# Second layer of an attention and expert kernel: the first rows ahead of the layer's start, v scaled by a constant, outputs in float16

## The chip, the cores and the metric

One core of a Trainium2 chip runs the whole program. The metric is the time of one execution on the device in microseconds (us); the kernel before takes 884.76 us, the median of three runs.

## The reference

```python
def reference(q, k, v, f, moe_*, moe2_*):
    x = decayed causal attention of q, k, v, f       # 4 batches, 8 heads, 576 rows, width 64
    x = x.transpose(...).reshape(4, 576, 512)
    u = x + (x.T @ U @ V).T                           # mixing of rows, rank 32
    y = u + max(u @ w_ch1, 0) @ w_ch2                 # 512 -> 2048 -> 512
    logits = y @ w_gate                               # 4 experts, the best two are kept
    for e in range(4):
        a = causal softmax(y @ wq[e] @ (y @ wk[e]).T / 8)
        out += weight[e] * (a @ (y @ wv[e]) @ wo[e])
```

All inputs are float32 and the result is wanted to nearly that accuracy. So each large product is made three times, from a high and a low half of both factors (high by high, high by low, low by high).

## The kernel before, in words

The program has three stages: the attention of the first layer (to about 200 us) and its row mixing, the feed-forward part, and the second layer, in which each of 4 batches has 4 expert heads (16 heads in all, from about 672 us on).

**Feed-forward.** The hidden width is worked in four quarters. A step is one quarter of one half (288 rows) of a batch. It makes 4 hidden tiles (`hps`, 12 matmuls of 288 columns each; ScalarE writes the high half `hh`, VectorE the low half `hl`), and the matmuls of step i's outputs (`cps`) alternate with the hidden tiles of step i+1. The input `ust` of a step is split in two parts (`cast_some`): ScalarE writes `uh`, and the low half `ul` is `ust` minus `uh`. The outputs of the last quarter, `yc`, are the second layer's input y. For each batch `largest_y` and `finish_y` look for the largest magnitude of y in each partition, turn the maximum over the partitions into a power of two, and write y times that factor as float16 halves `yh` and `yl` to `yhalves` in DRAM, from where `load_y` brings them in for the second layer. For batches 0 to 2 the maximum over the partitions goes through TensorE (`power`). For the last batch `power_aside` sends the 128 values to DRAM (`mdram`) and reads them back as a row in every partition (`mrow`).

**Second layer.** For a batch, `experts_qk(b, pair)` makes q and k of two heads (48 `pq` matmuls of 288 columns); ScalarE and VectorE each write one half of every result, times `back`, the product of the factors that were taken out. `expert_values` makes v and the gate's logits (60 `pv` matmuls of 260 columns). `head_max` makes the bound of each row's scores in three parts: products `ua`, products `ub`, and the transposition `mt`; it ends in a row `mr`, which is put by DMA beside q. A head's scores `sc` are made in two pieces, ScalarE takes their exponentials `pf`, GpSimd masks the diagonal (`affine_select`), ScalarE and VectorE split them into `ph` and `pl`, and one head later come the products `av` with v. `expert_out` transposes a batch's outputs (`op`), splits them in `oh` and `ol`, and makes the products `po` with wo (512 columns), which go out from `ost`.

**v in the kernel before.** ScalarE copies each `pv` to `vr` (L1340), VectorE takes the largest magnitude (`bm`, L1341). When all five tiles are there, `batch_scale` makes one power of two (`bsp`, `bs`), ScalarE scales the whole `vr` (L1319) and writes the high half `vh` (L1320), and GpSimd makes the low half `vl` in four subtractions (L1322).

**Order.** In the feed-forward part TensorE, VectorE and ScalarE (and the transfer queue of SyncE) execute the instructions in the order in which the program is written. In the second layer only TensorE does; the order on ScalarE, VectorE and GpSimd there is set by the framework's scheduler when the program is built. `work_on(n)` advances queued generators (`work`) by n pieces between the fixed parts of a head. A piece that ends in `LATER` is not counted, so several may follow in one place. Products with a result in PSUM take three buffers in turn (pool `psf`: `hps`, `cps`, `pq`, `pv`, `op`, `po`, `mt`), and two more are for `ua`, `ub` and `sc`. A matmul waits until its buffer has been read.

## Time and profile before

| | |
|---|---|
| median of 3 runs | 884.76 us (884.66 to 885.23) |
| profiled execution, its own time | 880.85 us |
| span of its trace | 878.7 us |
| TensorE clock granted, mean (1 is full) | 0.965 |
| busy: TensorE, VectorE, ScalarE, GpSimd | 89%, 73%, 50%, 28% of the span |
| last matmul ends, span ends | 874.7, 878.7 us |
| time by engine of the chain that ended last | TensorE 63%, VectorE 21%, DMA 8%, ScalarE 4% |

The span is the time from the first to the last instruction in the trace. It lies 2.15 us under that execution's own time, and the median of the three runs is 3.9 us above the profiled execution. Changes are therefore worked out in the trace and then taken from the median. In the rows, PE is TensorE, DVE VectorE, ACT ScalarE and POOL GpSimd; L1281 is line 1281 of the kernel; a tile's name stands as out<-in.

### The profile page before, as it was taken

How to read it: one execution, taken by the hardware profiler on the slowest of the kernel's cores; microseconds unless marked ns; L12 is line 12 of the kernel's file. 1: busy time of each engine (PE TensorE's matmuls, PEld its weight loads, DVE VectorE, ACT ScalarE, POOL GpSimd, SP SyncE). 2: the span in 40 equal slices, each digit the busy share in tenths (PEclk: the TensorE clock that was granted, in tenths of full speed). 3: DMA queues.
4: the chain of work that ended last, by engine and by line, in shares of the span. 5: the costliest groups of instructions: out<-in, count | busy, mean ns of one | idle time of the engine just before them, and what ended most of it. 6: DMA issues, size and time to landing. Idle time of an engine off the chain costs nothing.

```text
span 878.7 us, 19044 instructions
## 1 busy us (share of the span) xinstructions
PE 778.8 (89%) x7422; PEld 691.2 (79%) x7422; DVE 642.5 (73%) x1692; ACT 436.8 (50%) x824; POOL 242.3 (28%) x325
## 2 busy tenths in 40 slices
PE   3487487889999999989799999999998689989897
PEld 2477487888999899989799877777776478878786
DVE  6989978986777657646849873775663779877775
ACT  3668566555455554443417331332231367666764
POOL 9856645543433423000200001002004022121210
PEclk9889689999999999999999999999999799999999
DMA  6344565443443431116345323144010531422122
GB/s 185 108 114 137 179 201 164 124 135 96 133 117 91 139 111 48 57 49 208 129 125 184 118 84 116 29 162 151 1 54 1 174 85 27 106 60 66 43 72 84
DMA packets 56617, 93.75 MB, mean 107 GB/s; under 512 B 5024, under 2 KB 36240, under 8 KB 56528
## 3 DMA queue, kind: packets, MB, share of 16 engines
q1 hardware_dynamic: 51968, 83.76, 32.0%
q10 hardware_dynamic: 4560, 8.78, 2.7%
q8 instruction: 58, 0.95, 0.4%
q14 instruction: 31, 0.25, 0.1%
HBM read 53.32 MB, written 21.38 MB: 85 GB/s over the span
## 4 chain that ended last, share of the span: by engine, by line
PE 63%; DVE 21%; DMA 8%; ACT 4%; issue 3%; POOL 0%; SPq 0%; POOLq 0%; DVEq 0%; ACTq 0%
PE cps L634 19%; PE hps L618 18%; PE sc L231 7%; DVE ph L247 4%; PE pv L1337 3%; DVE ub L188 3%; PE po L1379 3%; DMA ust<-udram 2%; DMA raw<-in_w_dram 2%; PE ub L183 2%; PE pq L1266 2%; PE gp L828 2%; PE av L262 1%; PE av L266 1%; PE av L264 1%
## 5 line engine op out<-in xcount | busy, mean ns | idle before, releaser
L622 ACT ACTIVATE hh<-hps 128x288 fp32r<-128x288 f32 (+1 forms) x128 | 52.5, 410 | 208.9 <-PE hps L618 201.6
L247 DVE TENSOR_TENSOR ph<-pf,ph 128x576 f16<-128x576 f32 x144 | 129.0, 899 | 29.9 <-ACT ph L246 29.5
L623 DVE SCALAR_TENSOR_TENSOR hl<-hps,hh 128x288 fp32r<-128x288 f32 (+1 forms) x128 | 58.0, 453 | 76.8 <-ACT hh L622 76.5
L241 ACT ACTIVATE pf<-sc 128x576 f32<-128x576 f32 x144 | 84.1, 612 | 37.7 <-PE sc L231 30.5
L231 PE MATMUL sc<-qa,ka 128*128 128x288 f32 (+4 forms) x288 | 77.2, 329 | 21.8 <-DMA qa<-mr 10.1
L246 ACT CAST ph<-pf 128x576 f16<-128x576 f32 x144 | 89.3, 636 | 5.5 <-POOL pf L243 4.2
L188 DVE CUSTOM_DVE_ANT_0 ub<-ub,maskm 128x448 f32<-128x448 f32 x192 | 81.8, 426 | 11.1 <-PE ub L183 8.9
L634 PE MATMUL cps<-hh,w2h 128*128 128x288 f32 x256 | 79.7, 311 | 0.0
L618 PE MATMUL hps<-uh,w1h 128*128 128x288 f32 x256 | 75.1, 315 | 3.5 <-DVE hl L623 1.6
L634 PE MATMUL cps<-hh,w2l 128*128 128x288 f32 x256 | 76.0, 297 | 0.0
L634 PE MATMUL cps<-hl,w2h 128*128 128x288 f32 x256 | 75.8, 296 | 0.0
L231 PEld LDWEIGHTS sc<-qa,ka 128*128 128x128 f32 x288 | 53.5, 206 | 26.9 <-ACT pf L241 5.7
L262 PE MATMUL av<-vh,ph 128*128 128x65 f16 x720 | 72.3, 197 | 2.0 <-DVE x L311 2.0
L634 PE MATMUL cps<-hl,w2hf 128*128 128x288 f16 x256 | 73.2, 286 | 0.0
L634 PE MATMUL cps<-hh,w2lf 128*128 128x288 f16 x256 | 73.2, 286 | 0.0
L634 PE MATMUL cps<-hh,w2hf 128*128 128x288 f16 x256 | 73.2, 286 | 0.0
L264 PE MATMUL av<-vl,ph 128*128 128x64 f16 x720 | 71.9, 194 | 0.0
L266 PE MATMUL av<-vh,ph 128*128 128x65 f16 x720 | 71.8, 194 | 0.0
L262 PEld LDWEIGHTS <-ph 128*128 128x128 f16 x720 | 66.5, 98 | 5.7 <-DVE x L311 2.1
L618 PE MATMUL hps<-uh,w1l 128*128 128x288 f32 x256 | 71.0, 299 | 0.0
L231 PE MATMUL sc<-qb,kb 128*128 128x288 f32 (+4 forms) x288 | 68.3, 319 | 0.0
L264 PEld LDWEIGHTS <-ph 128*128 128x128 f16 x720 | 66.9, 100 | 0.2
(235 smaller groups left out, 2318.5 us busy)
## 6 DMA issues: line engine op xcount, KB each, us to landing
raw<-in_w_dram SPq DMA_DIRECT2D x32, 512.0 KB
qkt<-in_qk_dram SPq DMA_DIRECT2D x16, 576.0 KB
ust<-udram SPq DMA_DIRECT2D x14, 576.0 KB
vr<-in_v_dram SPq DMA_DIRECT2D x16, 320.0 KB
udram<-ustage ACTq DMA_DIRECT2D x16, 288.0 KB
ydram<-ust SPq DMA_DIRECT2D x8, 576.0 KB
yc<-ydram SPq DMA_DIRECT2D x8, 576.0 KB
qb<-qa SPq DMA_DIRECT2D x24, 144.0 KB
```

Of the source, the lines that this page charges most:

```text
L188: nc.vector.tensor_tensor_reduce(ub[:, bk, off:off + w], ub[:, bk, off:off + w], maskm[:, S - w:S], 1.0, NEG, OP.add, OP.max, mx[:, t:t + 1])
L231: nc.tensor.matmul(ps[:, bk, off:off + w], wa, xa, start=bk not in banks[:n], stop=bk not in banks[n + 1:])
L241: nc.scalar.activation(pfv, view, AF.Exp, scale=ISC)
L246: nc.scalar.copy(ph[:, o0:o0 + n], pf[:, 0:n])
L247: nc.vector.tensor_tensor(pl[:, o0:o0 + n], pf[:, 0:n], ph[:, o0:o0 + n], OP.subtract)
L262: nc.tensor.matmul(av[:, it, :], ph[:, c:c + P], vh[:, jt, :], start=first, stop=False)
L264: nc.tensor.matmul(av[:, it, 0:64], ph[:, c:c + P], vl[:, jt, :], start=False, stop=False)
L266: nc.tensor.matmul(av[:, it, :], pl[:, c:c + P], vh[:, jt, :], start=False, stop=last)
L618: nc.tensor.matmul(ph[:], wa[:, k, fs], xa[:, k], start=n == 0, stop=n == 3 * KT - 1)
L622: nc.scalar.activation(hh[:], ph[:], AF.Relu)
L623: nc.vector.scalar_tensor_tensor(hl[:], ph[:], 0.0, hh[:] if dt == F16 else f32(hh[:]), OP.max, OP.subtract)
L634: nc.tensor.matmul(pc[:], wa[:, t, dsl], xa[:], start=n == 0, stop=n == 3 * FT - 1)
```

## The change

1. `first_rows`: q and k of the first two heads and the row bounds of heads 0 and 1 are made in the last two feed-forward steps instead of behind them.
2. The last batch's y is not split in halves behind the feed-forward part. It is stored as it is (`ydram`), and `last_y` loads it in the second batch's heads (from head 5 on), takes the maximum there, and splits it in four pieces of 576 elements per partition on ScalarE (`yh`) and VectorE (`yl`). Its two small matmuls use the buffers of `psf`. `power_aside` goes.
3. v is scaled by the constant `DOWN`, 2 to the power of -22. ScalarE writes `vh` and the logits `lg` and VectorE writes `vl` for each tile straight from `pv`. The copy, the maximum, `batch_scale` and `batch_parts` go.
4. wo, `oh` and `ol` are float16; wo gets a scale of its own (a third `power`), which a factor in the scaling of `ost` takes back.
5. `cast_some` makes `ul` on VectorE instead of GpSimd.

```diff
+DOWN = 2.0 ** -22
...
-    def power_aside(am, up):
-
-        nc.sync.dma_start(mdram[:], am)
-        full = cur["s16"].tile([P, P], F32, name="mrow", bufs=1)
-        nc.sync.dma_start(full[:], mdram[:].rearrange("p o -> o p").to_broadcast([P, P]))
-        yield
-        es = cur["s16"].tile([P, 2], F32, name="es", bufs=16)
-        nc.vector.tensor_reduce(es[:, 0:1], full[:], AX.X, OP.max)
-        nc.vector.tensor_scalar(es[:, 0:1], es[:, 0:1], 1.0e-30, None, OP.max)
-        nc.vector.tensor_scalar(es[:, 0:1].bitcast(I32), es[:, 0:1].bitcast(I32), 0x7F800000, None,
-                                OP.bitwise_and)
-        nc.vector.tensor_scalar(es[:, 0:1], es[:, 0:1], 1.0 / up, None, OP.mult)
-        nc.vector.reciprocal(es[:, 1:2], es[:, 0:1])
-        return es
...
-            nc.gpsimd.tensor_tensor(dl, sv, f32(dh), OP.subtract)
+            nc.vector.tensor_tensor(dl, sv, f32(dh), OP.subtract)
...
-                if j == KT - 1 and q == 3:
+                if j == KT - 1 and q == 3 and b < B - 1:
...
-    woh = sw.tile([P, 2, DM], F32R, name="woh")
-    wol = sw.tile([P, 2, DM], F32R, name="wol")
+    woh = sw.tile([P, 2, DM], F16, name="woh")
+    wol = sw.tile([P, 2, DM], F16, name="wol")
...
+        parts = [(g, k, wah[:, k, c0:c1], wal[:, k, c0:c1], wraw[:, k, c0:c1])
+                 for k in range(KT) for g, (c0, c1) in enumerate(((0, q1), (q1, NA)))]
+        parts += [(2, k, woh[:, k, :], wol[:, k, :], sts[k][:]) for k in range(2)]
...
+        back, ey = backs[b], st_y[b][:, 0:1]
         for g in range(2):
-            nc.vector.tensor_tensor(backs[b][:, g:g + 1], st_y[b][:, 0:1], st_w[g][:, 0:1], OP.mult)
+            nc.vector.tensor_tensor(back[:, g:g + 1], ey, wscales[:, g:g + 1], OP.mult)
+        nc.vector.scalar_tensor_tensor(back[:, 2:3], back[:, 1:2], 1.0 / DOWN, wscales[:, 2:3],
+                                       OP.mult, OP.mult)
...
-    def batch_scale(am):
-
-        sp = psf.tile([P, NT], F32, name="bsp", tag="f")
-        nc.tensor.matmul(sp[:], every[:], am[:], start=True, stop=True)
-        rs = sy.tile([P, 1], F32, name="bs", bufs=4)
-        nc.vector.tensor_reduce(rs[:], sp[:], AX.X, OP.max)
-        nc.vector.tensor_scalar(rs[:], rs[:], 1.0 / VEXP, 1.0e-30, OP.mult, OP.max)
-        nc.vector.tensor_scalar(rs[:].bitcast(I32), rs[:].bitcast(I32), 0x7F800000, None,
-                                OP.bitwise_and)
-        nc.vector.reciprocal(rs[:], rs[:])
-        yield
-        return rs
-
-    def batch_parts(vr, rs, vh, vl):
-
-        scaled = nc.scalar.mul(vr, vr, rs[:, 0:1])
-        nc.scalar.copy(vh[:, :, :, 0:64], vr)
-        for e in range(E):
-            nc.gpsimd.tensor_tensor(vl[:, :, e], vr[:, :, e], vh[:, :, e, 0:64], OP.subtract)
-        return scaled
...
     def expert_values(b, y):
 
         yh, yl = y
-        vr = sy.tile([P, NT, NV], F32, name="vr3", bufs=1)
         v0 = 2 * E * D
-        am = sy.tile([P, NT], BF16, name="bm")
+        vh = sy.tile([P, NT, E, 65], F16, name="vh3")
+        vl = sy.tile([P, NT, E, 64], F16, name="vl3")
+        nc.gpsimd.memset(vh[:, :, :, 64:65], 1.0)
+        lg = sy.tile([P, NT, E], F32, name="lg3")
         for t in range(NT):
             pv = psf.tile([P, 512], F32, name="pv", tag="f")
             ts_ = slice(t * P, t * P + P)
...
                     nc.tensor.matmul(pv[:, 0:NV], ya[:, k, ts_], wa[:, k, v0:v0 + NV],
                                      start=n == 0, stop=n == 3 * KT - 1)
                     n += 1
-            nc.scalar.mul(vr[:, t, :], pv[:, 0:NV], backs[b][:, 1:2])
-            nc.vector.tensor_reduce(am[:, t:t + 1], vr[:, t, 0:E * D], AX.X, OP.max,
-                                    apply_absolute_value=True)
-            yield
-        vh = sy.tile([P, NT, E, 65], F16, name="vh3")
-        vl = sy.tile([P, NT, E, 64], F16, name="vl3")
-        nc.gpsimd.memset(vh[:, :, :, 64:65], 1.0)
-        vv_ = vr[:, :, 0:E * D].rearrange("p t (e d) -> p t e d", e=E)
-        yield LATER
-        scale = batch_scale(am)
-        next(scale)
-        yield LATER
-        rs = drain(scale)
-        st_v[b] = (vh, vl, rs, sy.tile([P, E, NT], F32, name="cf", bufs=2))
-        first = batch_parts(vv_, rs, vh, vl).ins
-        gating.append(gates(vr[:, :, E * D:NV], st_v[b][3]))
+            pe_ = pv[:, 0:E * D].rearrange("p (e d) -> p e d", e=E)
+            nc.scalar.mul(vh[:, t, :, 0:64], pe_, DOWN)
+            last = nc.scalar.mul(lg[:, t, :], pv[:, E * D:NV], backs[b][:, 1:2]).ins
+            nc.vector.scalar_tensor_tensor(vl[:, t], pe_, DOWN, vh[:, t, :, 0:64], OP.mult,
+                                           OP.subtract)
+            yield
+        st_v[b] = (vh, vl, sy.tile([P, E, NT], F32, name="cf", bufs=2))
+        gating.append(gates(lg[:], st_v[b][2]))
         if b == 0:
-            with tc.issue_after(first):
+            with tc.issue_after(last):
                 drain(gating.pop())
...
-        oh = sy.tile([P, 2, S], F32R, name="oh", bufs=1)
-        ol = sy.tile([P, 2, S], F32R, name="ol", bufs=1)
+        oh = sy.tile([P, 2, S], F16, name="oh", bufs=1)
+        ol = sy.tile([P, 2, S], F16, name="ol", bufs=1)
...
-            nc.scalar.copy(ost[0:k, :], po[0:k, :])
+            nc.scalar.mul(ost[0:k, :], po[0:k, :], backs[b][0:k, 2:3])
...
+    def last_y(yh, yl):
+
+        b = B - 1
+        halves = [sy.tile([P, KT, HC], F32, name=f"yst{c}", bufs=1) for c in range(NC)]
+        for c in range(NC):
+            nc.sync.dma_start(halves[c][:], ydram[b, :, :, c * HC:c * HC + HC])
+        for t_ in (yh, yl):
+            nc.gpsimd.memset(t_[:, :, S:SP_], 0.0)
+        yield LATER
+        yield LATER
+        am = sy.tile([P, 2 * NC], F32, name="yam", bufs=1)
+        for n in range(2 * NC):
+            k = 2 * (n % 2)
+            nc.vector.tensor_reduce(am[:, n:n + 1], halves[n // 2][:, k:k + 2], AX.XY, OP.max,
+                                    apply_absolute_value=True)
+            yield LATER
+        a1 = sy.tile([P, 1], F32, name="ya1", bufs=1)
+        nc.vector.tensor_reduce(a1[:], am[:], AX.X, OP.max)
+        yield LATER
+        st_y[b] = yield from power(a1[:], UPW, ((psf, "f"), (psf, "f")), LATER)
+        factors_back(b)
+        up = st_y[b][:, 1:2]
+        for c in range(NC):
+            cs = slice(c * HC, c * HC + HC)
+            for k in range(0, KT, 2):
+                dh, dl, sv = yh[:, k:k + 2, cs], yl[:, k:k + 2, cs], halves[c][:, k:k + 2]
+                nc.scalar.mul(dh, sv, up)
+                nc.vector.scalar_tensor_tensor(dl, sv, up, dh, OP.mult, OP.subtract)
+                yield LATER
...
+    def first_rows():
+
+        yield from experts_qk(0, 0, y)
+        yield
+        cur["first_k"] = cur["tmp"].ins
+        rows = [head_max(0), head_max(1)]
+        for m in (0, 1):
+            one(rows[m])
+            yield
+            one(rows[m])
+            yield
+        yield
+        for m in (0, 1):
+            one(rows[m])
+            yield
+
     NH = B * E
+    with tc.manual_schedule(engines=IN_ORDER):
+        jobs.append(second_weights())
+        y = load_y(0, sy0)
+        dense_until(len(steps) - 2)
+        drain(in_turn(*jobs))
+        del jobs[:]
+        for b in range(B - 1):
+            factors_back(b)
+        jobs.append(first_rows())
+        dense_until(len(steps))
+        drain(in_turn(*jobs))
+        del jobs[:]
...
     with tc.manual_schedule(engines={mybir.EngineType.PE}):
-        drain(experts_qk(0, 0, y))
-        first_k = cur["tmp"].ins
         work.append(experts_qk(0, 1, y))
+        work.append(expert_values(0, y))
+        sc = expert_scores(0, 0)
         work_on(2)
-        m0, m1 = head_max(0), head_max(1)
-        one(m0)
-        work_on(1)
-        one(m0)
-        work_on(1)
-        one(m1)
-        work.append(expert_values(0, y))
-        work_on(1)
-        one(m1)
-        work_on(1)
-        one(m0)
-        work_on(3)
-        one(m1)
-        with tc.issue_after(first_k):
+        one(sc)
+        work_on(2)
+        one(sc)
+        work_on(2)
+        with tc.issue_after(cur["first_k"]):
             y_next = load_y(1, ys[1])
         for h in range(NH):
             b, e = divmod(h, E)
             more = b + 1 < B
             if e == 0 and more:
+                if b + 2 == B:
+                    drain(late)
                 y = y_next
                 work.append(experts_qk(b + 1, 0, y))
-            if e == 1 and b + 2 < B:
+            if e == 1 and b + 2 < B - 1:
                 with tc.issue_after(cur["last"].ins):
                     y_next = load_y(b + 2, ys[b % 2])
+            if e == 1 and b + 2 == B - 1:
+                y_next = [ys[b % 2].tile([P, KT, SP_], F16, name=n) for n in ("yh", "yl")]
+                late = last_y(*y_next)
+                with tc.issue_after(cur["last"].ins):
+                    next(late)
+                work.insert(0, late)
```

Where the change moves instructions is read from the order of each engine's instructions, first on VectorE where the feed-forward part ends and the second layer begins. `yc` is the end of a feed-forward step, the lines with `qb` and `kb` write q and k of the first heads, `es<-mrow` is the last batch's power of two. The kernel before:

```order
L639 SCALAR_TENSOR_TENSOR yc<-cps,back,yc 128x288 x4
L531 TENSOR_REDUCE yam<-yc 128x1 x2
L555 TENSOR_REDUCE ya_9148<-yam 128x1
L1281 SCALAR_TENSOR_TENSOR qb_8332<-pq,back_8320,qa_8331 64x288
L1281 SCALAR_TENSOR_TENSOR qb_8336<-pq,back_8320,qb_8336 64x288
L1281 SCALAR_TENSOR_TENSOR qb_8332<-pq,back_8320,qa_8331 64x288
L543 TENSOR_REDUCE es<-mrow 128x1
L1281 SCALAR_TENSOR_TENSOR qb_8336<-pq,back_8320,qb_8336 64x288
L544 TENSOR_SCALAR es<-es 128x1
```

The changed kernel:

```order
L613 SCALAR_TENSOR_TENSOR hl<-hps,hh 128x288
L1251 SCALAR_TENSOR_TENSOR qb_8332<-pq,back_8320,qa_8331 64x288
L1251 SCALAR_TENSOR_TENSOR qb_8336<-pq,back_8320,qb_8336 64x288
L629 SCALAR_TENSOR_TENSOR yc<-cps,back,yc 128x288
L1251 SCALAR_TENSOR_TENSOR qb_8332<-pq,back_8320,qa_8331 64x288
L1251 SCALAR_TENSOR_TENSOR qb_8336<-pq,back_8320,qb_8336 64x288
L613 SCALAR_TENSOR_TENSOR hl<-hps,hh 128x288
L1251 SCALAR_TENSOR_TENSOR kb_8334<-pq,back_8320,ka_8333 64x288
L1251 SCALAR_TENSOR_TENSOR kb_8338<-pq,back_8320,tmp 64x288
```

The work on the first q and k now stands between `hl` and `yc` of the feed-forward steps, and no instruction that reads `mrow` stands among it.

On ScalarE in the second batch's heads, where q and k of the third batch are made (`qa`, `qb`, `ka`, `tmp`), the kernel before has the two long steps on v:

```order
L1284 ACTIVATE qa_9202<-pq,back_8322 64x288
L241 ACTIVATE pf<-sc 128x512 x2
L1286 ACTIVATE qb_9207<-pq,back_8322 64x288
L1319 ACTIVATE vr_10362<-vr_10362,bs 128x5x256
L246 CAST ph_9238<-pf 128x512
L1284 ACTIVATE qa_9202<-pq,back_8322 64x288
L246 CAST ph_9238<-pf 128x512
L1320 CAST vh_10541<-vr_10362 128x20x64
L1293 ACTIVATE ka_9204<-pq,back_8322 64x288
L1286 ACTIVATE qb_9207<-pq,back_8322 64x288
```

The changed kernel has the four pieces of the last batch's y (`yh<-yst`) there, in the middle of the same eight instructions of q and k:

```order
L1254 ACTIVATE qa_9304<-pq,back_8322 64x288
L1256 ACTIVATE qb_9309<-pq,back_8322 64x288
L1385 ACTIVATE yh<-yst_10278,es 128x2x288 x2
L1385 ACTIVATE yh<-yst_10279,es 128x2x288 x2
L1254 ACTIVATE qa_9304<-pq,back_8322 64x288
L1263 ACTIVATE ka_9306<-pq,back_8322 64x288
L241 ACTIVATE pf<-sc 128x576
L246 CAST ph_9342<-pf 128x576
L1263 ACTIVATE ka_9306<-pq,back_8322 64x288
```

The two steps on v are gone from between the reads of `pq`, and four steps on y stand in one row between the first and the second pair of them.

On VectorE at about 419 to 436 us, where the feed-forward weights of a later quarter are prepared (`w`, `wam`), the changed kernel has the subtractions `ul` in its row, which in the kernel before are GpSimd's:

```order
L613 SCALAR_TENSOR_TENSOR hl<-hps,hh 128x288
L599 TENSOR_TENSOR ul<-ust,uh 128x576
L352 SCALAR_TENSOR_TENSOR w_5791<-raw,w_5791 128x512
L353 SCALAR_TENSOR_TENSOR w_5791<-raw,w_5791 128x512
L438 TENSOR_REDUCE wam<-w_5791 128x1
L627 TENSOR_TENSOR ust<-cps,ust 128x288
L599 TENSOR_TENSOR ul<-ust,uh 128x576
```

Each `ul` stands ahead of the next weights, and behind it wait the low halves `hl` that TensorE needs.

## Rows read from the trace of the kernel before

**Rows 1.** Page, part 1: busy time of each engine, share of the span, instructions.

```profile
PE 778.8 (89%) x7422; PEld 691.2 (79%) x7422; DVE 642.5 (73%) x1692; ACT 436.8 (50%) x824; POOL 242.3 (28%) x325
```

**Rows 2.** Windows: from:to, length, busy time of each engine (instructions), TensorE clock, DMA.

```profile
570.00:664.00 94.00, 94.00 (x774) 75.07 (x773) 60.46 (x142) 28.56 (x58) 5.40 (x13) 1.00 0.25 86
...
678.00:687.00 9.00, 0.00 (x0) 0.00 (x0) 0.81 (x2) 0.35 (x1) 0.00 (x0) 0.62 0.22 56
687.00:703.00 16.00, 13.39 (x95) 10.23 (x96) 14.75 (x43) 8.51 (x16) 0.56 (x2) 0.90 0.68 209
703.00:719.00 16.00, 13.07 (x103) 11.04 (x101) 13.04 (x46) 11.57 (x21) 4.82 (x11) 0.96 0.16 35
719.00:723.00 4.00, 4.00 (x26) 3.30 (x24) 2.28 (x5) 1.97 (x4) 0.29 (x1) 0.74 0.63 154
723.00:779.00 56.00, 51.77 (x625) 45.31 (x624) 49.99 (x157) 40.61 (x73) 14.63 (x40) 1.00 0.30 73
779.00:783.00 4.00, 3.98 (x19) 3.68 (x20) 3.34 (x11) 1.96 (x7) 0.29 (x1) 0.57 0.35 76
...
827.00:831.00 4.00, 4.00 (x20) 3.93 (x21) 3.22 (x12) 2.13 (x5) 0.29 (x1) 0.59 0.34 74
```

**Rows 3.** Chain that ended last: start, us, engine or DMA, tile, line, count.

```profile
674.03 7.35 DMA mdram<-ya
681.40 4.71 DMA mrow<-mdram
687.03 4.72 PE pq L1266 x24
...
783.62 1.48 PE po L1379 x6
...
814.13 1.49 PE pq L1266 x12
```

**Rows 4.** Waits of PE, 671 to 879: total us, times, longest.

```profile
PE pq L1266 <- DVE qb L1281: 9.2, 1, 9.2
PE op L1368 <- DVE qb L1281: 3.4, 2, 1.7
PE mt L193 <- DVE qb L1281: 2.9, 1, 2.9
...
PE op L1368 <- DVE kb L1281: 2.0, 2, 1.0
```

**Rows 5.** Timeline of DVE: start, duration, line, operation, tiles, idle before.

```profile
686.13 0.29 DVE L543 TENSOR_REDUCE es<-mrow 128x1 f32<-128x128 f32 x1 [9.96 <-DMA mrow<-mdram]
```

**Rows 6.** Timeline of ACT, where the second batch's heads run, columns as in group 5.

```profile
771.16 1.36 ACT L1319 ACTIVATE vr<-vr,bs 128x1280 f32<-128x1280 f32 x1
...
773.96 1.26 ACT L1320 CAST vh<-vr 128x1280 f16<-128x1280 f32 x1
```

**Rows 7.** Timeline of DVE at the same place.

```profile
776.09 0.74 DVE L307 TENSOR_TENSOR rn<-rn,cf 128x5 f32<-128x5 f32 x1
```

**Rows 8.** Timeline of POOL at the same place.

```profile
775.31 2.98 POOL L1322 TENSOR_TENSOR vl<-vr,vh 128x320 f16<-128x320 f32 x4 [4.13 <-ACT vh L1320]
```

**Rows 9.** Groups of instructions, 703 to 879: count, busy us, mean ns, idle before.

```profile
L1341 DVE TENSOR_REDUCE bm<-vr 128x1 bf16<-128x256 f32 x19 | 7.9, 417 | 2.8 <-ACT vr L1340 2.4
```

**Rows 10.** Groups of instructions, 640 to 680, columns as in group 9.

```profile
L623 DVE SCALAR_TENSOR_TENSOR hl<-hps,hh 128x288 f16<-128x288 f32 x9 | 4.1, 457 | 8.3 <-ACT hh L622 8.3
...
L566 DVE SCALAR_TENSOR_TENSOR yl<-yc,es,yh 128x576 f16<-128x576 f32 x4 | 3.3, 814 | 0.0
...
L565 ACT ACTIVATE yh<-yc,es 128x576 f16<-128x576 f32 x4 | 3.0, 771 | 1.3 <-DVE es L405 1.3
```

**Rows 11.** A window, as in group 2, in the feed-forward part.

```profile
430.00:435.00 5.00, 4.29 (x34) 4.06 (x33) 4.90 (x9) 3.21 (x6) 2.81 (x2) 1.00 0.00 0
```

**Rows 12.** Timeline of DVE in that window.

```profile
432.83 1.93 DVE L348 SCALAR_TENSOR_TENSOR w<-raw,w 128x512 int32<-128x512 int32 x1
434.79 0.69 DVE L349 SCALAR_TENSOR_TENSOR w<-raw,w 128x512 int32<-128x512 int32 x1
```

More of the change, by code (lines that the diff above doesn't have):

```diff
@@ L146 @@
     ydram = dram.tile([B, P, KT, S], F32, name="ydram")
-    mdram = dram.tile([P, 1], F32, name="mdram")
     yhalves = dram.tile([B, 2, P, KT, S], F16, name="yhalves")
@@ L386, in load_quarter_steps, with power @@
             yield
-    def power(am, up=UP16):
-        at_ = ps1.tile([1, P], F32, name="amt", tag="av")
+    def power(am, up=UP16, where=((ps1, "av"), (ps2, "s2")), pause=None):
+        (p0, tag0), (p1, tag1) = where
+        at_ = p0.tile([1, P], F32, name="amt", tag=tag0)
         nc.tensor.transpose(at_[:], am, ident[:])
@@ L398, in power @@
                                 OP.bitwise_and)
-        yield
-        yield
-        rp = ps2.tile([P, 1], F32, name="rsp", tag="s2")
+        yield pause
+        yield pause
+        rp = p1.tile([P, 1], F32, name="rsp", tag=tag1)
         nc.tensor.matmul(rp[:], every[:], full[:].bitcast(BF16)[:, 1:2], start=True, stop=True)
@@ L557, in finish_y @@
         yield
-        es = yield from (power_aside if b == B - 1 else power)(a1[:], UPW)
+        es = yield from power(a1[:], UPW)
         up = es[:, 1:2]
@@ L1133 @@
     wal = sw.tile([P, KT, NA], F16, name="wal")
-    woh = sw.tile([P, 2, DM], F32R, name="woh")
-    wol = sw.tile([P, 2, DM], F32R, name="wol")
-    backs = [sw.tile([P, 2], F32, name=f"back{b}") for b in range(B)]
+    woh = sw.tile([P, 2, DM], F16, name="woh")
+    wol = sw.tile([P, 2, DM], F16, name="wol")
+    wscales = sw.tile([P, 3], F32, name="wscales")
+    backs = [sw.tile([P, 3], F32, name=f"back{b}") for b in range(B)]
     wide = pool("wide")
@@ L1171, in part @@
                     lambda: nc.vector.scalar_tensor_tensor(dl, sv, up, dh, OP.mult, OP.subtract))
-        yield from behind_by_one([part(k, g) for k in range(KT) for g in range(2)])
-        for k in range(2):
-            nc.scalar.copy(woh[:, k, :], sts[k][:])
-            yield
-            nc.vector.tensor_tensor(wol[:, k, :], sts[k][:], f32(woh[:, k, :]), OP.subtract)
+        yield from behind_by_one([pair(*part) for part in parts])
     def factors_back(b):
+        back, ey = backs[b], st_y[b][:, 0:1]
         for g in range(2):
-            nc.vector.tensor_tensor(backs[b][:, g:g + 1], st_y[b][:, 0:1], st_w[g][:, 0:1], OP.mult)
+            nc.vector.tensor_tensor(back[:, g:g + 1], ey, wscales[:, g:g + 1], OP.mult)
+        nc.vector.scalar_tensor_tensor(back[:, 2:3], back[:, 1:2], 1.0 / DOWN, wscales[:, 2:3],
+                                       OP.mult, OP.mult)
     tie = sw.tile([P, E, E], F32, name="tie")
@@ L1197, in load_y @@
         return yh, yl
-    with tc.manual_schedule(engines=IN_ORDER):
-        jobs.append(second_weights())
-        y = load_y(0, sy0)
-        dense_until(len(steps) - 1)
-        for b in range(B - 1):
-            factors_back(b)
-        dense_until(len(steps))
-    drain(in_turn(*jobs))
-    factors_back(B - 1)
-    wide.release()
-    for p_ in (y16, s16, fy, fh, fu, wy_pool, wx_pool, stage):
-        p_.release()
-    hpool2 = pool("heads3", 1, "right")
-    att = pool("att2", 2, "right")
-    cur["pf"] = att
-    sy = pool("sy", 2, "right")
-    ys = [sy0, pool("sy1", 1, "right")]
-    heads += make_heads(hpool2, NH2B)
-    fill_heads(heads[NH2A:])
-    exps = exponent_tiles(hpool2, 2)
     def gates(lg, cf):
@@ L1397, in last_out @@
     def last_out(b):
-        oh = sy.tile([P, 2, S], F32R, name="oh", bufs=1)
-        ol = sy.tile([P, 2, S], F32R, name="ol", bufs=1)
+        oh = sy.tile([P, 2, S], F16, name="oh", bufs=1)
+        ol = sy.tile([P, 2, S], F16, name="ol", bufs=1)
         osum = sy.tile([P, NT, DM], F32, name="osum", bufs=1)
@@ L1407, in last_out @@
                 if m == 0:
-                    nc.scalar.copy(osum[0:k, t, :], po[0:k, :])
+                    nc.scalar.mul(osum[0:k, t, :], po[0:k, :], backs[b][0:k, 2:3])
                 else:
-                    nc.vector.tensor_tensor(osum[0:k, t, :], po[0:k, :], osum[0:k, t, :], OP.add)
+                    nc.vector.scalar_tensor_tensor(osum[0:k, t, :], po[0:k, :], backs[b][0:k, 2:3],
+                                                   osum[0:k, t, :], OP.mult, OP.add)
                     queue = nc.scalar if t % 2 else nc.sync
@@ L1498 @@
                 work.append(tail)
[L1499 removed]
+            if h:
+                sc = expert_scores(b, e)
             m = head_max(h + 2) if h + 2 < NH else iter(())
```

49 lines of the change are left out of this document (30 added, 19 removed).

## The prediction

> **What bounds the kernel now.** I read the page first: TensorE is busy 89% of the span [rows 1], so the question is where it pauses, and whether this change is at those places. The chain that ended last answers for the start of the second layer. For most of the feed-forward part it is TensorE's own products, and then comes a stretch with no engine in it: 7.35 us of a transfer to `mdram`, 4.71 us of one back as `mrow`, and only then 24 products `pq` [rows 3]. VectorE stands at the instruction that reads `mrow` for 9.96 us [rows 5]; behind it in the program's order are the reads of `pq`, so TensorE waits 9.2 us for a `qb` that needs nothing of `mrow` [rows 4]. The windows show the price: from 678 to 687 TensorE does nothing, and from 687 to 703 it has 13.39 us of work in 16 at a granted clock of 0.90 [rows 2].
>
> The list of TensorE's waits names three more places of the kind: a product waits for its PSUM buffer, which a read of q or k still holds. `op` waits for `qb` twice (3.4 us) and for `kb` twice (2.0), and `mt` once for `qb` (2.9) [rows 4]. The windows at 719, 779 and 827 have a clock of 0.74, 0.57 and 0.59, each right behind such a wait [rows 2]: TensorE was idle, and then ran for some time at the lower of its two levels (1.2 instead of 2.4 GHz). What makes `qb` late is seen on ScalarE and VectorE at about 771 to 777. ScalarE has 1.36 us on `vr` and 1.26 us on `vh` [rows 6], VectorE one operation of 5 elements that takes 0.74 us [rows 7] while GpSimd subtracts `vl` for 2.98 us [rows 8], and q and k stand in line behind them.
>
> **The change part by part.** The sum is over what TensorE loses or works less; all differences are of the profiled execution and are then taken from the median.
>
> *Start of the layer.* Lost now: 9.0 us idle, 16 - 13.39 = 2.6 idle, and 16 x 0.10 = 1.6 at the low clock [rows 2], 13.2 in all. Afterwards nothing reads `mrow`, 48 of the 96 first `pq` products and the bounds of heads 0 and 1 lie inside the last two feed-forward steps, and the first scores can follow the last `cps` at once. The work itself is only moved. What it needs of VectorE there is 8 reads of `pq`, each like an `hl` (0.46 [rows 10]), and the bounds, together some 8 us as an estimate; from 570 to 664 VectorE was busy 60.46 of 94 us [rows 2], so the last two steps have room for it. I leave 0.5 us for a seam, so **-12.7**. If the cover is gone, that is if these reads make TensorE pause in the last steps, the gain sinks towards nothing; that end is a rival.
>
> *v.* The three pauses for `qb` and `kb` cost 3.4 + 2.0 + 2.9 = 8.3 us idle [rows 4] and 4 x (0.26 + 0.43 + 0.41) = 4.4 at the low clock [rows 2], so 12.7. The change takes away what stands in the line: 2.6 us of ScalarE in two blocks, 20 reductions of 0.417 on VectorE [rows 9], 2.98 on GpSimd. It adds `vl` on VectorE, 20 of 256 elements. The nearest row is `hl` of 288 elements, also from PSUM with a subtraction, 0.457 [rows 10], so 0.42 each: VectorE has as much as before. ScalarE has about 0.2 us more per tile for the logits, spread out. I take all three pauses as gone, **-12.7**; the lower end is that they stay, nothing.
>
> *The last batch's y.* Its four ScalarE pieces are of 0.77 us, its four VectorE pieces of 0.81 [rows 10], and its four reductions I take as no longer than these. That is 3.1 us of ScalarE in one row between reads of `pq` in the second batch's heads, the same kind of block that 1.36 + 1.26 us make now. I therefore put one pause back: 3.5 us (the four pieces, and an opening on VectorE) and 4 x 0.43 = 1.7 at the low clock, **+5.2**. The lower end is nothing, when the pieces find a gap. Its load from DRAM is 1.2 MB in a stretch in which the DMA engines are 16 to 30% busy [rows 2] and has several us of room; I cost it at nothing, and it would add its own lateness if head 5 came before it.
>
> *float16 outputs.* A `po` product has 512 columns; six take 1.48 us now, 0.247 each [rows 3]. Float16 products of 288 columns run at 1.49 / 12 = 0.124 [rows 3], so 512 at the same pace take 0.221. 120 of them and the small rest give 120 x 0.026 = **-3.1**. The bounds are no gain and that.
>
> *`ul` on VectorE.* Each is 576 elements, near the 0.81 of `yl` [rows 10], and four come into a stretch in which VectorE is busy 4.90 of 5 us and TensorE 4.29 [rows 11]. At worst all is on the path: +3.2. Against it stands that one weight operation took 1.93 us beside GpSimd's `ul`, while its neighbour of the same size took 0.69 [rows 12]; that 1.2 comes back. I also count some lateness, since `ul` waits in VectorE's order for the landing of `ust` which held up GpSimd alone before: **+1.5**, bounds -1.2 and +4.
>
> The Trainium skill ("SBUF — State Buffer", section "Who interferes with whom") says that VectorE with two inputs in SBUF and GpSimd reading SBUF exclude each other for a whole instruction. The 1.93 us and the 0.74 us above agree. By that rule up to 1.4 us (half of 2.81) could come back at each of four casts, 5.6 instead of 1.2, and the edit would be a gain of some 3 us, for 858.6 in all. The trace shows the collision at one cast, so I stay with +1.5 and give that a tenth of the main case's chance.
>
> The sum: -12.7 - 12.7 + 5.2 - 3.1 + 1.5 = -21.8. With 884.76 that is 863.0. The profiled execution is 880.85, 3.9 under the median, and the changed kernel may have another such distance.
>
> **The rivals.** (1) *VectorE bounds the second layer.* From 723 to 779 it is busy 49.99 of 56 us, hardly less than TensorE's 51.77 [rows 2]. The change takes 7.9 us of reductions off it and adds 8.4 of `vl`, 3.3 of `yl`, 3.3 of reductions of y. Then the pauses go from v to other places, and only the start counts: 884.8 - 12.7 - 3.1 + 1.5 = 870.5, and 873.6 if `po` gains nothing. Against it: TensorE's waits of the second layer that I list are all for q and k behind ScalarE's long steps, not spread over heads. (2) *No pause for the last y.* The scheduler put the pieces where `pq` has buffers to spare: 863.0 - 5.2 = 857.8, or 856 if small waits go as well. (3) *The start isn't covered.* The first q, k and bounds hold up the feed-forward steps by as much as they save: 863.0 + 12.7 = 875.7. (4) *Slower.* With v's maximum gone, every tile of v needs two ScalarE steps and one of VectorE before its PSUM buffer is free, where one copy was enough. If that makes TensorE pause in each of heads 1 to 11 as it does now in three of them, at 12.7 / 3 = 4.2 us, 11 pauses cost 46 us. The rest of the change saves 12.7 + 12.7 + 3.1 - 1.5 = 27, so it decides from the seventh such pause on; with eight the time is 884.8 - 27 + 34 = 892. For it speaks how full VectorE is, against it that each tile has 12 products of its own, which cover such a read. (5) *It does nothing*: one of start and v fails and the other is paid back; I see no single place for it.
>
> **How the numbers follow.** Main case 0.53, 863 with its own range 857 to 868 (the pause of y from 2 to 8 us, `ul` by its bounds). Rival 1 0.21, rival 2 0.15, rival 3 0.05, rival 4 0.04, rival 5 0.02. For 8 in 10 the range needs the main case, rival 2, and most of rival 1: 854 to 873. A measurement of this kernel can tell about 0.2% from no change, 1.8 us. Faster by more: 0.94; within: 0.02; slower: 0.04.
>
> **What the profile of the changed kernel would show.** *Start:* no idle stretch of TensorE between the last `cps` and the first scores, clock 1.00 throughout; idle time before `cps` or `hps` in the last 30 us would speak for rival 3. *v:* no `op` or `mt` waiting for `qb` or `kb` in the first and third batches' heads, and no window of 4 us under 0.9 there. *Last y:* one wait of `pq` or of what follows it for ScalarE's `qa`, `qb` or `ka`, 2 to 4 us, in the second batch's heads, and a window near 0.6 behind it. *`po`:* six in about 1.33 us. *`ul`:* TensorE busy less than 4.2 of 5 us near 430. Wrong would be the forecast above all if VectorE is busy more than 95% in the second layer while TensorE pauses in many heads.

## The result and the profile after

Of the changed kernel four runs gave a median of 873.51 us (867.55 to 874.85), against 884.71 (883.14 to 885.23) for the kernel before: a ratio of 0.986, 95% interval 0.982 to 0.991. Six further runs beside 17 of the kernel before, on another occasion, gave 0.982 (0.979 to 0.986). By these ratios it is faster by 12 to 16 us (the medians differ by 11.2 and 16.8), and 21.8 were forecast. The profiled execution took 873.55 us; its span is 871.8.

The page's first part hardly differs from [rows 1], busy time of each engine with its share of the span:

```profile
PE 782.5 (90%) x7422; PEld 689.9 (79%) x7422; DVE 640.1 (73%) x1695; ACT 428.6 (49%) x836; POOL 223.9 (26%) x305
```

The windows answer to [rows 2] (columns as there). First the end of the feed-forward part with the start of the second layer, then two pairs of windows in the second batch's heads:

```profile
664.00:678.00 14.00, 14.00 (x117) 11.19 (x115) 7.71 (x24) 5.19 (x11) 0.00 (x0) 1.00 0.28 76
678.00:687.00 9.00, 9.00 (x75) 7.42 (x74) 7.36 (x27) 0.41 (x1) 3.60 (x10) 1.00 0.15 33
687.00:700.00 13.00, 13.00 (x110) 10.92 (x108) 6.69 (x15) 6.49 (x15) 6.51 (x21) 1.00 0.57 160
752.00:756.00 4.00, 1.59 (x21) 1.26 (x18) 3.95 (x10) 0.71 (x2) 0.00 (x0) 1.00 0.17 35
756.00:760.00 4.00, 3.38 (x17) 2.56 (x17) 3.11 (x16) 0.97 (x4) 0.00 (x0) 0.57 0.35 74
772.00:776.00 4.00, 2.69 (x20) 2.27 (x19) 3.94 (x11) 3.54 (x9) 0.90 (x2) 1.00 0.25 53
776.00:780.00 4.00, 2.66 (x12) 2.57 (x13) 3.84 (x8) 3.26 (x7) 1.57 (x4) 0.61 0.36 80
```

From 664 to 700 TensorE is never idle and its clock is 1.00: the hole at the start is gone. But there are two pauses in the second batch's heads, with VectorE busy 3.95 of 4 us in the first, and a low clock behind each.

TensorE's waits from 400 us on (total, times, longest), where [rows 4] had the waits for `qb` and `kb`:

```profile
PE hps L608 <- DVE ust L627: 4.5, 1, 4.5
PE pv L1288 <- DVE vl L1294: 3.0, 1, 3.0
PE op L1311 <- DVE qb L1251: 2.7, 1, 2.7
PE po L1322 <- ACT oh L1312: 1.4, 2, 1.0
PE ub L183 <- ACT ka L1263: 1.4, 1, 1.4
PE op L1311 <- DVE ol L1313: 1.3, 1, 1.3
```

The first line is not in the second layer but in the feed-forward part; the kernel before had 0.9 us of this wait, in two pieces. The next two are the two pauses of the windows. The others are small and new.

Medians of a few runs don't settle terms of 3 to 10 us here, since two runs of one kernel differ by up to 12 (876.2 to 887.8 for the kernel before on one occasion). The trace does, by marks that every execution has. I took the starts of the 128 `hl` of the feed-forward part; these are the rows of the 17th, 41st, 49th, 55th and 128th in the changed kernel's timeline of VectorE:

```profile
237.67 0.45 DVE L613 SCALAR_TENSOR_TENSOR hl<-hps,hh 128x288 fp32r<-128x288 f32 x1
...
387.15 0.44 DVE L613 SCALAR_TENSOR_TENSOR hl<-hps,hh 128x288 fp32r<-128x288 f32 x1
...
434.10 0.45 DVE L613 SCALAR_TENSOR_TENSOR hl<-hps,hh 128x288 fp32r<-128x288 f32 x1
...
455.30 0.46 DVE L613 SCALAR_TENSOR_TENSOR hl<-hps,hh 128x288 fp32r<-128x288 f32 x1 [1.57 <-ACT hh L612]
...
680.75 0.46 DVE L613 SCALAR_TENSOR_TENSOR hl<-hps,hh 128x288 f16<-128x288 f32 x1 [1.00 <-ACT hh L612]
```

The differences between such marks, and from the last to the span's end, for every kernel of this study (us):

| kernel | 1st to 17th | 41st to 49th | 55th to 128th | 128th to end |
|---|---|---|---|---|
| before | 109.3 | 43.0 | 219.1 | 213.6 |
| changed | 114.6 | 47.0 | 225.4 | 191.1 |
| after_again | 107.6 | 46.5 | 225.5 | 191.6 |
| casts_gpsimd | 112.1 | 43.9 | 225.5 | 189.9 |
| ymax_early | 113.2 | 49.0 | 225.5 | 187.3 |
| first_behind | 111.8 | 49.4 | 219.2 | 206.3 |
| v_measured | 111.4 | 47.6 | 225.5 | 203.2 |
| casts_lag | 107.3 | 42.9 | 225.5 | 190.8 |
| spread | 112.1 | 45.4 | 225.5 | 191.5 |
| spread_gpsimd | 110.5 | 43.5 | 225.5 | 189.9 |
| lag_ymax | 113.0 | 43.0 | 225.5 | 187.4 |
| no_last_y | 109.7 | 47.9 | 225.5 | 183.9 |
| out_f32r | 110.1 | 47.8 | 225.5 | 193.9 |

The first column is chance: up to there each engine has the same instructions in the same order in every one of these kernels, and it runs from 107.3 to 114.6. What differs is TensorE's granted clock. These are the windows from the 1st to the 17th `hl` in the shortest (casts_lag) and in the longest (the changed kernel):

```profile
122.82:230.12 107.30, 94.92 (x999) 89.55 (x998) 89.99 (x230) 65.18 (x124) 54.06 (x35) 1.00 0.49 150
123.03:237.67 114.64, 102.23 (x1000) 96.94 (x1000) 92.46 (x229) 65.04 (x124) 53.07 (x35) 0.93 0.46 140
```

TensorE's busy time for the same products grows by 7.3 us, which is the whole difference. The third column repeats to 0.1 us. It is 6.4 longer with the first q, k and bounds in it; that is work moved out of the fourth. The fourth repeats less well: the changed kernel, after_again and casts_gpsimd have the same instructions there in the same order and take 191.1, 191.6 and 189.9, with TensorE idle for 16.4, 16.4 and 16.3. The 1.7 us between them are again clock (the last section shows where), so a difference of under 2 us in this column shows nothing, and I compare with the range 189.9 to 191.6. In the last two columns together the changed kernel gains 16.2 us (432.7 to 416.5; 15.6 and 17.4 in the other two).

In the second column it loses 4.6 in the mean of the eight executions that have `ul` on VectorE right behind `uh` (47.6). Part of this is chance as well: the step from the 41st to the 42nd `hl` takes either 13.2 or 14.5 to 14.7 us, in kernels of both kinds. Clear of that are the two steps from the 47th to the 49th: 13.2 to 15.7 us in these eight, in the mean 14.4, and 10.2 to 11.3, in the mean 10.8, in the five others. So `ul` there costs 3.6 us.

### The profile page after: what moved, and what is told of

Same layout as the page of the kernel before. It is cut to its first block, busy times and chain, and to the rows that moved or that the text cites. A ratio compares the mean times of both kernels' runs of the same rounds, so it can differ in the third digit from the quotient of the medians.

```text
span 871.8 us, 19040 instructions
## 1 busy us (share of the span) xinstructions
PE 782.5 (90%) x7422; PEld 689.9 (79%) x7422; DVE 640.1 (73%) x1695; ACT 428.6 (49%) x836; POOL 223.9 (26%) x305
## 4 chain that ended last, share of the span: by engine, by line
PE 67%; DVE 19%; DMA 7%; issue 3%; ACT 3%; SPq 1%; POOL 0%; DVEq 0%; POOLq 0%; ACTq 0%
PE cps L624 20%; PE hps L608 19%; PE sc L231 7%; DVE ph L247 4%; PE pq L1236 4%; PE pv L1288 3%; PE po L1322 3%; DMA ust<-udram 2%; DVE ub L188 2%; PE ub L183 2%; PE gp L818 2%; DMA raw<-in_w_dram 2%; PE av L262 2%; PE av L266 1%; PE av L264 1%
## 5 line engine op out<-in xcount | busy, mean ns | idle before, releaser
L612 ACT ACTIVATE hh<-hps 128x288 fp32r<-128x288 f32 (+1 forms) x128 | 52.4, 409 | 209.5 <-PE hps L608 191.5
```

Of the source, the lines that this page charges most:

```text
L612: nc.scalar.activation(hh[:], ph[:], AF.Relu)
```

## The experiments

The theory before them: the start and v gain what was forecast, and the rest is lost in two places, `ul` on VectorE and the last batch's y. "Undone" is said of the changed kernel.

**The changed kernel again (after_again).** No edit.

> The changed kernel once more, to see how far the changed kernel's own runs differ. The two traces differ by 5.3 us before 257 us, where the order of the instructions on every engine is the same in both kernels. If that is chance between runs, this trace has the 17th hl of the feed-forward part anywhere between 232 and 238 us and the ratio to before is 0.984 to 0.988; if it comes with the change (other addresses in memory), it stands near 237.7 us again.

The 17th `hl` stood 107.6 us behind the first instead of 114.6, and at 228.5 us below even the range that I expected of chance; the ratio was 0.982, also below it. Chance between runs, then; the 5.3 us by which the two profiled executions part ahead of 257 us belong to no edit.

**`ul` back on GpSimd (casts_gpsimd).**

```diff
-            nc.vector.tensor_tensor(dl, sv, f32(dh), OP.subtract)
+            nc.gpsimd.tensor_tensor(dl, sv, f32(dh), OP.subtract)
```

> The changed kernel with the four subtractions ul back on GpSimd. Theory 1: on VectorE they wait for the landing of ust with the hl behind them, which costs 3.6 us between the 41st and the 49th hl; without them the time falls by 3 to 4 us (ratio about 0.982) and TensorE's 4.5 us wait of hps for ust goes. Rival: ust lands late in both, ScalarE's uh holds up hh as well, and the time stays within 1 us of the changed kernel.

The stretch from the 41st to the 49th `hl` went to 43.9, 3.7 us less than that mean of 47.6, its last two steps to 10.2, and the wait of `hps` for `ust` is down to the 0.9 us of the kernel before. The ratio is the expected 0.982 (0.979 to 0.985), but after_again has the same without the edit, so the ratio shows nothing; the first part, which scatters by 7 us, hides it. The steps show it.

**`ul` one place later on VectorE (casts_lag).**

```diff
+        if cur.get("half"):
+            dh, dl, sv = cur.pop("half")
+            nc.vector.tensor_tensor(dl, sv, f32(dh), OP.subtract)
         if casts:
-            dh, dl, sv = casts.pop(0)
+            dh, dl, sv = cur["half"] = casts.pop(0)
             nc.scalar.copy(dh, sv)
-            nc.vector.tensor_tensor(dl, sv, f32(dh), OP.subtract)
```

> The changed kernel with each ul still on VectorE, but issued at the next place of cast_some, one product group after its uh. Theory: not the 0.76 us of an ul costs but the wait in VectorE's order for ust and uh with hl behind it; one place later most of that wait is over, and the stretch from the 41st to the 49th hl (46.5 to 49.4 us in four runs with ul on VectorE, 43.0 and 43.9 on GpSimd) comes to 43 to 45.5. Rival: VectorE's time counts in a stretch in which it is nearly full; then it stays over 46.5.

42.9 us, as with GpSimd, with the same four subtractions on VectorE (one execution; lag_ymax below has 43.0). The timelines show it. The changed kernel, VectorE, then ScalarE:

```profile
420.92 0.43 DVE L613 SCALAR_TENSOR_TENSOR hl<-hps,hh 128x288 fp32r<-128x288 f32 x1
426.12 0.76 DVE L599 TENSOR_TENSOR ul<-ust,uh 128x576 fp32r<-128x576 f32 x1 [4.76 <-ACT uh L598]
...
430.14 0.44 DVE L613 SCALAR_TENSOR_TENSOR hl<-hps,hh 128x288 fp32r<-128x288 f32 x1
```

```profile
425.42 1.24 ACT L598 CAST uh<-ust 128x576 fp32r<-128x576 f32 x2 [4.89 <-DMA ust<-udram]
```

And casts_lag, VectorE:

```profile
411.51 0.43 DVE L615 SCALAR_TENSOR_TENSOR hl<-hps,hh 128x288 fp32r<-128x288 f32 x1
...
416.00 0.76 DVE L598 TENSOR_TENSOR ul<-ust,uh 128x576 fp32r<-128x576 f32 x1 [1.65 <-ACT uh L601]
...
418.14 0.46 DVE L615 SCALAR_TENSOR_TENSOR hl<-hps,hh 128x288 fp32r<-128x288 f32 x1 [1.11 <-ACT hh L614]
```

`ust` lands late in both (in casts_lag ScalarE waits 4.19 us for it). But with `ul` ahead in VectorE's order, nothing of VectorE's own goes on: 4.76 us of standing, and from this `hl`, the 47th, to the next 9.2 us instead of 6.6. It is the wait, not the 0.76.

**The maxima of the last y earlier (ymax_early).** The four reductions are taken from `yc` in the last feed-forward steps, and `last_y` goes straight from the reload to `power`.

```diff
...
+                    if q == 3:
+                        jobs.append(largest_last(yc, c))
...
-        for n in range(2 * NC):
-            k = 2 * (n % 2)
-            nc.vector.tensor_reduce(am[:, n:n + 1], halves[n // 2][:, k:k + 2], AX.XY, OP.max,
-                                    apply_absolute_value=True)
-            yield LATER
...
```

> The changed kernel with the maxima of the last batch's y taken from yc at the end of the feed-forward steps, and only the splitting left to the second batch's heads. Theory 1: the four reductions there, the first of which waits for the reload, were what held up kb and vl; the waits of 1.2 and 3.0 us at about 751 to 757 and the low clock behind them (1.7) go, 4 to 6 us in all (ratio about 0.981). Rival: VectorE is full in these heads, and the pause comes back in another place, less than 2 us gained.

187.3 instead of 189.9 to 191.6 behind the last `hl` (187.4 in lag_ymax): 2.6 to 4.3 us, at or under the lower end of what was expected. TensorE's idle time there falls by 3.0 us, from 16.4 to 13.4. The ratio, 0.983 (0.979 to 0.987), says nothing here either. The changed kernel's timelines of VectorE, then ScalarE, show what held it up:

```profile
749.96 1.41 DVE L1372 TENSOR_REDUCE yam<-yst 128x1 f32<-128x576 f32 x2 [0.92 <-DMA yst<-ydram]
...
753.32 1.41 DVE L1372 TENSOR_REDUCE yam<-yst 128x1 f32<-128x576 f32 x2
...
754.73 0.50 DVE L1251 SCALAR_TENSOR_TENSOR kb<-pq,back,ka 64x288 fp32r<-64x288 f32 x1
...
756.16 0.41 DVE L1294 SCALAR_TENSOR_TENSOR vl<-pv,vh 128x256 f16<-128x256 f32 x1
```

```profile
755.26 0.50 ACT L1265 ACTIVATE tmp<-pq,back 64x288 fp32r<-64x288 f32 x1 [3.67 <-DVE kb L1251]
```

Two pairs of reductions (1.41 each, and 0.92 of waiting) stand ahead of `kb`; ScalarE waits 3.67 us for `kb`, with `vh` behind, and `vl` comes at 756.16, when TensorE has stood 3.0 us for its buffer.

**The last y left out (no_last_y).** The third batch's halves are loaded in place of the last batch's: no reload, no maximum, no splitting.

```diff
-        for b in range(B - 1):
+        st_y[B - 1] = st_y[B - 2]
+        for b in range(B):
             factors_back(b)
...
-                y_next = [ys[b % 2].tile([P, KT, SP_], F16, name=n) for n in ("yh", "yl")]
-                late = last_y(*y_next)
+                late = iter(())
                 with tc.issue_after(cur["last"].ins):
-                    next(late)
-                work.insert(0, late)
+                    y_next = load_y(b + 1, ys[b % 2])
```

> The changed kernel without the last batch's y: the third batch's halves are loaded a second time in their place, so the reload, the maximum and the splitting of the last batch's y are left out (the last batch's result is that of other data). Theory: both pauses of the second batch's heads (waits of 3.0 and 2.7 us, idle time around them, and low clock behind each) belong to that work, 9 to 11 us, and the stretch behind the last hl falls from 191.3 to 180 to 182.5 us. Forecast's own term: one pause of 5.2, so 186. Rival: VectorE is full in these heads without it too, and the stretch stays over 188.

183.9 (one execution): the work on the last y costs 6.0 to 7.7 us (189.9 to 191.6, less 183.9), 4.6 of them idle time of TensorE, more than the forecast's one pause of 5.2 and less than the 9 to 11 of the theory. Both pauses went, but a small one came in their place: TensorE's waits after 640 us here begin with

```profile
PE op L1311 <- DVE ol L1313: 2.6, 2, 1.3
PE po L1322 <- ACT oh L1312: 1.4, 2, 1.0
PE ub L183 <- ACT ka L1263: 1.4, 1, 1.4
```

where the changed kernel has `op` waiting for `ol` once.

**The pieces of the last y apart (spread).** In addition to ymax_early, the power of two is made in the first batch's heads, and the four pieces are two places apart.

```diff
...
+            if h == 1:
+                work.insert(0, last_scale())
...
                 nc.scalar.mul(dh, sv, up)
                 nc.vector.scalar_tensor_tensor(dl, sv, up, dh, OP.mult, OP.subtract)
                 yield LATER
+                yield LATER
```

> The changed kernel with the maxima of the last y in the feed-forward steps, its power of two in the first batch's heads, and the four pieces of the splitting apart. Theory: both pauses of the second batch's heads go; the stretch behind the last hl falls from 191.3 (187.3 with the maxima alone moved) to 182 to 185 us. Rival: the pieces hold up another q or k wherever they stand; then it stays at 186 to 189.

191.5: all that ymax_early had gained is lost again (ratio 0.983, 0.979 to 0.986). The rival's mechanism held, and the loss is larger than its figure (186 to 189). With nothing left to wait for but the reload, ScalarE's order had the pieces between the reads of `pq` of the first pair of heads instead, two and two:

```profile
744.93 1.44 ACT L1396 ACTIVATE yh<-yst,eslast 128x576 f16<-128x576 f32 x2 [0.71 <-DMA yst<-ydram]
746.40 0.50 ACT L1276 ACTIVATE tmp<-pq,back 64x288 fp32r<-64x288 f32 x1
...
747.56 0.49 ACT L1274 ACTIVATE ka<-pq,back 64x288 fp32r<-64x288 f32 x1
...
748.47 1.44 ACT L1396 ACTIVATE yh<-yst,eslast 128x576 f16<-128x576 f32 x2
```

**The same with `ul` on GpSimd (spread_gpsimd).** Both edits together.

> The same with ul on GpSimd as before the change. If both parts count apart from each other, its stretch from the 41st to the 49th hl is 43 to 44 us and the one behind the last hl as in the kernel with the pieces apart, some 10 us in all under the changed kernel (ratio to before 0.971 to 0.975). If only chance between runs is seen in the feed-forward part, the ratio is that of the kernel with the pieces apart.

43.5 and 189.9: `ul` counts here as it does alone, but since the spreading gained nothing the sum stayed short of 10 us; ratio 0.978 (0.974 to 0.981), above the expected 0.971 to 0.975. The 1.6 us between this 189.9 and the 191.5 of spread are within what the column scatters.

**v's scale measured again (v_measured).** `batch_scale`, `batch_parts` and the copy `vr` as in the kernel before, so the undone edit is the part of the diff from `batch_scale` to `expert_values`; `back[:, 2:3]` then holds wo's scale alone.

> The changed kernel with v's scale measured as before: the copy to vr, the maximum, the two long steps of ScalarE and GpSimd's four subtractions per batch. Theory: the three pauses of the kernel before (8.3 us idle and 4.4 at the low clock) came from these steps, so at least the two in the first and third batches' heads come back, and the stretch behind the last hl of the feed-forward part (191.1 and 191.6 us in two runs of the changed kernel) becomes 199 to 204 us. Rival: VectorE bounds the second layer and v's part gained nothing; then it stays within 2 us of 191.3.

203.2, so in the changed kernel v's part is worth 11.6 to 13.3 us (ratio 0.996, 0.994 to 0.998: undone, some three quarters of the change's gain are gone). The long steps are back, and waits with them:

```profile
PE op L1333 <- DVE kb L1246: 4.8, 3, 2.5
PE mt L193 <- DVE cf L1210: 4.0, 1, 4.0
PE ub L183 <- ACT ka L1258: 2.6, 1, 2.6
PE av L262 <- ACT vh L1285: 1.7, 1, 1.7
PE av L264 <- POOL vl L1287: 0.7, 1, 0.7
```

They are not all the waits of the kernel before, though. `mt` does not wait for `qb` again; in its place `av` waits for `vh` and `vl`, and `mt` waits 4.0 us for `cf`, which it did nowhere before. So this run prices v's steps in the new order, and not the three pauses of [rows 4].

**The first rows behind the feed-forward part (first_behind).** The order of the kernel before there, with no transfer of a maximum.

```diff
-        jobs.append(first_rows())
         dense_until(len(steps))
-        drain(in_turn(*jobs))
-        del jobs[:]
...
+        drain(experts_qk(0, 0, y))
+        first_k = cur["tmp"].ins
         work.append(experts_qk(0, 1, y))
+        work_on(2)
+        m0, m1 = head_max(0), head_max(1)
...
```

> The changed kernel with the first q and k and the bounds of heads 0 and 1 behind the feed-forward part, in the order that the kernel before had. Nothing reads a maximum over partitions there any more. Theory 1: the wait for the transfer of the last batch's maximum was most of the start's loss of 13.2 us (9.2 idle and the low clock, 10.8), so this version loses only 2 to 4 us against the changed kernel (ratio about 0.990). Rival: it is the cover by the feed-forward steps that counts, and without it 8 to 13 us are lost (ratio 0.996 or more).

The stretches from the 55th `hl` to the end come to 425.5 instead of 415.3 to 417.1: 8.4 to 10.2 us lost (ratio 0.994, 0.992 to 0.997). That is the rival's figure. It isn't the rival's mechanism alone, though. I counted from the 55th `hl` to the first normalised output `o` of head 0. It is 281.2 us before, 270.5 in first_behind, 260.5 in the changed kernel, of which 4.0 are 36 products `pv` that it makes later. So without the transfer 10.7 us are gained there, and the cover by the feed-forward steps adds 6.0; but first_behind loses some 3 us again further on. The 10.7 are not the transfer's alone: the splitting of the last y, which in the kernel before stood ahead of a `kb` (TensorE waited 2.1 us for it), and v's long steps are gone there too, and no run parts the three. Its longest waits after 640 us, of which the 2.9 of `ua` and 2.0 of the first line come before that `o`:

```profile
PE mt L193 <- DVE mx L188: 5.8, 3, 2.5
PE mt L193 <- DVE ol L1313: 5.5, 2, 4.1
PE ua L171 <- DMA ka<-tmp: 2.9, 1, 2.9
```

**Outputs in 32 bits (out_f32r).** `woh`, `wol`, `oh` and `ol` as F32R.

> The changed kernel with wo, oh and ol in the 32-bit form as before, the rest as it is. Theory: 120 products po take 0.247 instead of 0.215 us each, and the stretch behind the last hl gets 3 to 4 us longer, 194 to 195.5. Rival: the products lie where TensorE waits anyhow for VectorE or ScalarE, and it stays under 192.5.

193.9 (one execution), so float16 is worth 2.3 to 4.0 us, against the expected 3 to 4. The products themselves do what was expected: six take 1.29 us in the changed kernel (864.77 to 866.06) where they took 1.48 [rows 3]. That would be 3.8 over 120 of them, which this range holds.

**Both mends together (lag_ymax).** casts_lag and ymax_early.

> The changed kernel with both mends that moved a stretch: ul one place later on VectorE, and the maxima of the last y taken in the feed-forward steps. Theory: they lie in different stretches and add up; from the 41st to the 49th hl 42.9 us (46.5 to 49.4 in the changed kernel), behind the last hl 187.3 (191.3), so the time is 8 us under the changed kernel's, ratio to before 0.970 to 0.978. Rival: one of them was a chance of its run, and the ratio stays at 0.98 or more.

43.0 and 187.4, each as alone; median 861.0 us, ratio 0.975 (0.971 to 0.980). This version beats both kernels, the changed one by some 8 us in the two stretches (its ratio is 0.007, or 6 us, below that of after_again).

## Why the prediction was right, and where it was off

The direction was right, the size too large by 6 to 10 us of 22; the median of 873.5 lies half a us above the upper end of the range, and the second occasion's ratio of 0.982 puts it at 869, inside. Step by step:

- **Start, forecast -12.7.** Right in mechanism and size. At the first output of head 0 the changed kernel is 20.7 us ahead, less 4.0 of `pv` made later. What v's part brings up to there has to be taken off as well: it is 2.2 by v_measured, which is so far behind the changed kernel there, or 4.0 by the wait of `mt` for `qb` and the low clock behind it [rows 4] [rows 2]. That leaves 12.7 to 14.5. Both halves count, the transfer and the cover.
- **v, -12.7.** Undone, it costs 11.6 to 13.3, but this agreement is in part luck, since the waits are others than the three that I priced. The windows of TensorE up to its last product say what became of those: the kernel before from 703 on, then the changed kernel, no_last_y and v_measured, each from the last `hl` on.

```profile
703.00:874.71 171.71, 160.20 (x1671) 136.85 (x1669) 136.25 (x425) 114.60 (x210) 34.70 (x102) 0.97 0.25 65
680.75:867.64 186.89, 174.67 (x1816) 140.63 (x1814) 147.67 (x458) 114.48 (x236) 32.15 (x112) 0.98 0.27 73
674.55:854.25 179.70, 172.09 (x1814) 138.30 (x1812) 141.75 (x441) 112.00 (x232) 31.11 (x112) 1.00 0.28 76
678.18:877.18 199.00, 180.05 (x1820) 144.52 (x1818) 152.48 (x473) 122.88 (x224) 44.38 (x128) 0.96 0.26 68
```

TensorE is idle for 11.5 us before, for 12.2 in the changed kernel, for 7.6 without the last y and for 18.9 with v measured. So with the last y's work left out it is idle for 3.9 us less than before, where I had taken 8.3 us of waiting as gone. The 4.4 of low clock did go: in no_last_y the clock is 1.00. That makes some 8.3 instead of 12.7. Rival 1 said that VectorE bounds the second layer, that the pauses go to other places, and that v gains nothing. Its price is refuted; that waits go to other places came true in part.
- **The last y, +5.2.** Mis-sized: 6.0 to 7.7. I priced one pause, behind ScalarE's four pieces, and gave the four reductions on VectorE and the wait for the reload none. They made a pause of their own.
- **float16, -3.1.** 2.3 to 4.0: right, as far as the scatter lets one see.
- **`ul` on VectorE, +1.5.** Mis-sized: +3.6 on the mean, near the upper bound that I gave it. I priced the instruction and the collision with GpSimd and left little for lateness; it was the lateness that cost. By the rule of the Trainium skill ("SBUF — State Buffer", section "Who interferes with whom") the edit would have gained 3 us, as the forecast estimated. The collision is there: the weight operation of 1.93 us [rows 12] takes 1.93 again in casts_gpsimd, and none in that part takes over 0.75 in the changed kernel. But it decides little: the stretch from the 49th to the 55th `hl`, in which it lies, takes 21.1 with `ul` on GpSimd, 21.2 with `ul` right behind `uh`, and 20.8 in casts_lag.
- **What the terms leave.** Counted like this, start, v, the last y and float16 make -12.7 - 8.3 + 7 - 3 = -17, with rough middles for the last two, and the last two columns show -15.6 to -17.4. With `ul` that is some -13. The runs in which one part was undone add up to more, about -22 (start 14.5, v 12, the last y 7, float16 3), since undoing one part also makes waits that the kernel before did not have, as v_measured shows. Which wait took the place of which is read from the lists: `op` waits 1.3 us for `ol` in the third batch's heads, where 2.7 were lost to `qb` and `kb` together; `ub` waits 1.4 for `ka` and `po` 1.4 for `oh`, and the list of the kernel before has no such waits. That these are late because others are gone is argued; no run shows it.

So the step of the prediction that was too hopeful is "I take all three pauses as gone", 8.3 us of waiting, where 3.9 us of idle time went. Two smaller ones are small work in front of a `pq` read (the reductions of y) and an instruction in front of `hl` (`ul`), both priced without what they would wait for.

## What to carry to other kernels

An instruction that is moved to an engine with a fixed order brings its wait along: ask what lands late in front of it and what stands behind it, before its duration; one place later in the same order it cost nothing here, and 3.6 us were saved. When the work that delays a buffer's reader is removed, price the next thing in that reader's line, not zero. And where runs scatter by 10 us for reasons ahead of the change, compare stretches between marks that both traces have. They repeated to 0.1 us where TensorE was never idle, and to 1.7 us where it paused, so look at the granted clock of both traces before you read a difference of 2 us.
